# Loads that cast, half-width turns and a re-ordered start in an attention and MLP kernel

## The chip, the core and the metric

The kernel runs on one core of a Trainium2 chip. A core has five engines that run on their own: PE (TensorE, matrix products), ACT (ScalarE), DVE (VectorE), POOL (GpSimd) and SP (SyncE, which here only issues transfers). Sixteen DMA engines move data between the memory of the chip and the core. The metric is the time of one execution in microseconds of device time. The kernel before takes 445.65 us, the median of three runs (445.64 to 447.6).

## The reference

```python
def _attn_ref(q, k, v):                     # (8, 12, 448, 64) each, float32
    S = q.shape[2]
    scale = 1.0 / np.sqrt(q.shape[-1])
    scores = scale * np.matmul(q, k.transpose(0, 1, 3, 2))
    attn = np.maximum(scores, 0.0) ** 2 / S
    return np.matmul(attn, v)

def _moe_ref(x, w_in, w_out, alpha):        # x (3584, 768), d_ff 2048
    h = x @ w_in
    g = np.maximum(h, 0.0) + alpha * np.minimum(h, 0.0)
    return g @ w_out
```

Attention with a squared relu in place of a softmax, over 8 batches of 12 heads, gives x with one row per token; a two-layer MLP with a leaky relu whose slope is given per column follows. Inputs and output are float32 in memory; the products run in bf16.

## The kernel before

Twelve heads of a batch are worked in three groups of four heads, called quads: quad n is group n % 3 of batch n // 3, and there are 24. For a quad, q, k and v are loaded by SP as float32 into `raw` tiles (three buffers each), cast to bf16 by POOL (quad 0's k by ACT and q by DVE), and q and k are turned so that the head dimension lies on the partitions. For quads 0 to 5 the turn is done on PE: seven matmuls of 128x128 with an identity into PSUM (`tps`, L117) and a DVE copy (L119). For later quads a transposing DMA on SP does it.

`scores(n, j)` makes block j (of 7) of a quad's scores in two PSUM banks with four 64x64 matmuls (`sc`, L137); ACT, or DVE for block 3 of the first six quads, takes the relu (`rl`), and DVE squares it (`at`, L147). `attnv(n)` multiplies the seven squares with v (`av`, L157), and ACT copies the result, scaled, into `xT`. Two double banks of PSUM (`scps`) are shared by scores and `av`; four single banks (`mmps`) by everything else.

`ffn1(b, ff)` is one of 16 steps of the first MLP half for batch b: six matmuls (`hps`, L173), a relu of the negative on ACT (`neg`), and one DVE instruction that writes `gT`. `ffn2` is the second half: 16 matmuls (`ops`, L185) give 128 rows by 384 columns, DVE copies them (`osb`, L191), and SP stores them. Batches go in pairs for `ffn2`: an even batch has 6 such groups, an odd one 8.

The order of the work on each engine is the order of the program; nothing reorders it. A quad's attention is cut into four bursts: burst 0 is one block of scores and the `attnv` of the quad before, bursts 1 to 3 are two blocks of scores each. `spread(seq, bursts)` sets bursts among MLP steps so that they are evenly spaced by a written cost (1.12 for an `ffn1` step, 2.6 for an `ffn2` group). Bursts of quads 6 and later also issue the load of quad n+3 (burst 0), the transposing DMAs of quad n+1 (burst 1) and the casts of quad n+2 (burst 2).

The start is written out: SP loads quads 0 to 2 and alpha; attention of batch 0 runs with no MLP work beside it; POOL issues the loads of `w_in` (which cast to bf16 in flight) between its casts. Then `ffn1` of batch 0 runs, with quad 3 among its last steps; quads 4 and 5 follow alone; then 14 steps of `ffn1` of batch 1 alone. From there bursts are spread over `ffn1` of batch b and `ffn2` of batch b-1, and the last batch's MLP ends the program.

Of the kernel before, what the change touches and what calls it, by code (L numbers as in the profile page):

```python
# [10 lines left out]
F32 = mybir.dt.float32  # L11
BF16 = mybir.dt.bfloat16
# [7 lines left out]
PP = 64  # L20
NJ = 7
# [3 lines left out]
def kernel(  # L25
# [27 lines left out]
    raw_pool = pool("raw", 3)  # L53
    cast_pool = pool("cast", 2)
    v_pool = pool("vp", 3)
    qkT_pool = pool("qkT", 2)
    rl_pool = pool("rl", 3)
    at_pool = pool("at", 10)
# [6 lines left out]

    w_in_sb = singles.tile([128, NG, 2, d_ff], BF16)
    w_out_sb = singles.tile([128, KF, d_model], BF16)
    alpha_sb = singles.tile([128, KF], F32)
    beta_sb = singles.tile([128, KF], F32)
    ident = singles.tile([128, 128], BF16)  # L70

    quads = [(b, g) for b in range(B) for g in range(NG)]
# [2 lines left out]
    raw, cast, qT, kT, vb = {}, {}, {}, {}, {}  # L75
    src = {"q": q, "k": k, "v": v}

    def load(n, names="qkv", after=None):
        b, g = quads[n]
        for w in names:  # L80
            t = raw_pool.tile([128, 2, NJ, D], F32, tag=w, name=f"{w}raw")
            raw[(n, w)] = t
            if after is not None:
                nc.gpsimd.tensor_copy(t[:, 0, 0, 0:1], after)
                after = None
            flat = src[w][b, 4 * g:4 * g + 4].rearrange("(s hf) (pp j) d -> (hf pp) s (j d)", hf=2, j=NJ)
            nc.sync.dma_start(out=t.rearrange("p s j d -> p s (j d)"), in_=flat)  # L87

    def copy(eng, o, i):
        if eng is nc.scalar:  # L90
# [4 lines left out]
    def to_bf16(n, w, eng):  # L95
        r = raw.pop((n, w))
        if w == "v":
            t = v_pool.tile([128, 2, NJ, D], BF16, tag="v", name="vb")
            vb[n] = t
            copy(eng, t, r)  # L100
        else:
            t = cast_pool.tile([128, NJ, 2, D], BF16, tag=w, name=f"{w}b")
            cast[(n, w)] = t
            copy(eng, t.rearrange("p j s d -> p s j d"), r)

    def transpose(n, w):
        store = qT if w == "q" else kT
        t = cast.pop((n, w))
        dst = qkT_pool.tile([128, NJ, 2, PP], BF16, tag=w, name=f"{w}T")
        store[n] = dst  # L110
        if n >= n_pe:
            nc.sync.dma_start_transpose(out=dst.rearrange("p j h c -> p j (h c)"),
                                        in_=t.rearrange("p j s d -> p (j s d)"))
            return
        ps = mm_ps.tile([128, NJ, 2, PP], BF16, tag="mm", name="tps")
        for j in range(NJ):
            nc.tensor.transpose(ps[:, j].rearrange("p h c -> p (h c)"),  # L117
                                t[:, j].rearrange("p s d -> p (s d)"), ident)
        nc.vector.tensor_copy(dst, ps)  # L119

    w_in_v = moe_w_in.rearrange("(g hf e pp) f -> hf e pp g f", hf=2, e=2, pp=64)
    w_out_v = moe_w_out.rearrange("(kf p) d -> p kf d", p=128)
# [5 lines left out]
                                    in_=w_in_v[hf, e, :, :, lo:hi])  # L128


    att, xT = {}, {}

    def scores(n, j):
        ps = sc_ps.tile([128, 2, 512], F32, tag="sc", name="sc")
        for r in range(2):
            for c in range(2):
                nc.tensor.matmul(ps[64 * c:64 * c + 64, r, :S],  # L137
                                 kT[n][64 * r:64 * r + 64, j, c, :],
                                 qT[n][64 * r:64 * r + 64, :, c, :],
                                 start=True, stop=True)  # L140
        rl = rl_pool.tile([128, 2, S], BF16, tag="rl", name="rl")
        if (n, j) in relu_on_dve:
            nc.vector.tensor_scalar(rl, ps[:, :, :S], 0.0, None, ALU.max)  # L143
        else:
            nc.scalar.activation(rl, ps[:, :, :S], ACTF.Relu)  # L145
        a = at_pool.tile([128, 2, S], BF16, tag="at", name="at")
        nc.vector.tensor_tensor(a, rl, rl, ALU.mult)  # L147
        att[(n, j)] = a

    def attnv(n):  # L150
        b, g = quads[n]
# [11 lines left out]
        nc.scalar.activation(xT[b][:, g], ps[:, :, :S], ACTF.Copy, scale=out_scale)  # L163


    gT, o_sb = {}, {}

    def ffn1(b, ff):
        if b % 2 == 0 and ff == 0:
# [12 lines left out]
    def ffn2(sb, c, hf):  # L182
        ps = mm_ps.tile([128, 384], F32, tag="mm", name="ops")
        for ff in range(KF):
            nc.tensor.matmul(ps, gT[sb][:, ff, bass.ts(c, 128)],  # L185
                             w_out_sb[:, ff, bass.ts(hf, 384)],
                             start=(ff == 0), stop=(ff == KF - 1))
        if hf == 0:
            o_sb[(sb, c)] = o_pool.tile([128, d_model], F32, tag="o", name="osb")
        o = o_sb[(sb, c)]  # L190
        nc.vector.tensor_copy(o[:, bass.ts(hf, 384)], ps)  # L191
        if hf == 1:
            for u in range(2):
                blk = 2 * c + u
                b, j = 2 * sb + blk // NJ, blk % NJ
                rows = out[b * S:(b + 1) * S].rearrange("(pp j) d -> j pp d", j=NJ)
                nc.sync.dma_start(out=rows[j], in_=o[64 * u:64 * u + 64])

    def steps(b, what):
        if what == "in":  # L200
            return [(1.12, lambda ff=ff: ffn1(b, ff)) for ff in range(KF)]
        cs = range(0, 3) if b % 2 == 0 else range(3, 7)
        return [(2.6, lambda c=c, hf=hf: ffn2(b // 2, c, hf)) for c in cs for hf in range(2)]


    NQ = len(quads)
    relu_on_dve = {(n, 3) for n in range(2 * NG)}

    def burst(n, i):

        if i == 0:
            if n < NQ:
                scores(n, 0)
            if (n - 1, 0) in att:
                attnv(n - 1)
        elif n < NQ:
            scores(n, 2 * i - 1)
            scores(n, 2 * i)
        if n < 2 * NG:
            return  # L220

        if i == 0 and n + 3 < NQ:
            load(n + 3)
        if i == 1 and n + 1 < NQ:
            transpose(n + 1, "k")
            transpose(n + 1, "q")
        if i == 2 and n + 2 < NQ:
            for w in "kqv":
                to_bf16(n + 2, w, nc.gpsimd)

    def spread(seq, bursts, share=0.92):

        total = sum(c for c, _ in seq) * share
        done, n = 0.0, 0
        for cost, fn in seq:
            while n < len(bursts) and done >= total * n / len(bursts):
                burst(*bursts[n])
                n += 1
            fn()
            done += cost  # L240
        assert n == len(bursts)


    for n in range(NG):
        load(n, "kqv")
    nc.sync.dma_start(out=alpha_sb, in_=moe_alpha.rearrange("(kf p) -> p kf", p=128))
    make_identity(nc, ident)
    for n in range(NG):
        to_bf16(n, "k", nc.gpsimd if n else nc.scalar)
        to_bf16(n, "q", nc.gpsimd if n else nc.vector)  # L250
        to_bf16(n, "v", nc.gpsimd)
        if n == 1:
            load_w_in(0, 512)
        if n < 2:
            transpose(n, "k")
            transpose(n, "q")
        if n > 0:
            for i in range(4):
                burst(n - 1, i)
    for i in range(1, 4):  # L260
        load_w_in(512 * i, 512 * i + 512)
    transpose(2, "k")
    transpose(2, "q")
    for i in range(4):
        burst(2, i)
    nc.vector.tensor_scalar(beta_sb, alpha_sb, -1.0, 1.0, ALU.mult, ALU.add)
    attnv(2)


    load(3, "kqv", after=w_in_sb[:, 0, 1, 1024:1025])  # L270
    load(4, "kqv")
    load(5, "kqv")
    for w in "kqv":
        to_bf16(3, w, nc.gpsimd)
    for w in "kqv":
        to_bf16(4, w, nc.gpsimd)
    for h in range(2):
        nc.gpsimd.dma_start(out=w_out_sb[:, 8 * h:8 * h + 8], in_=w_out_v[:, 8 * h:8 * h + 8])
    mlp = steps(0, "in")
    for _, fn in mlp[:9]:  # L280
        fn()
    transpose(3, "k")
    transpose(3, "q")
    for w in "kqv":
        to_bf16(5, w, nc.gpsimd)
    load(6, "kqv", after=w_out_sb[:, 0, 0:1])
    load(7, "kqv")
    load(8, "kqv")
    spread(mlp[9:], [(3, i) for i in range(4)])
    for n in (4, 5):  # L290
        transpose(n, "k")
        transpose(n, "q")
        for i in range(4):
            burst(n, i)
    attnv(5)
    for n in (6, 7):
        for w in "kqv":
            to_bf16(n, w, nc.gpsimd)
    for w in "kq":
        transpose(6, w)  # L300


    work = [(n, i) for n in range(2 * NG, NQ) for i in range(4)] + [(NQ, 0)]
    mlp = steps(1, "in")
    for _, fn in mlp[:14]:
        fn()
    spread(mlp[14:] + steps(0, "out") + steps(1, "out") + steps(2, "in"), work[:25])
    for b in range(3, B - 1):
        spread(steps(b, "in") + steps(b - 1, "out"), work[12 * b - 11:12 * b + 1])
    for _, fn in steps(B - 1, "in") + steps(B - 2, "out") + steps(B - 1, "out"):  # L310
        fn()


# [28 lines left out]
```

## Time and profile before

| What | Value |
|---|---|
| median of three runs | 445.65 us |
| the profiled execution | 447.29 us, of which 445.5 us lie between its first and last instruction (the span) |
| PE busy | 400.6 us, 90% of the span |
| DVE / ACT / POOL busy | 245.7 / 227.6 / 84.0 us |
| mean granted PE clock | 0.965 |
| read from / written to the chip's memory | 45.62 MB / 11.01 MB |

The page of the profile gives an engine's busy time, the span in 40 slices, the chain of waits that ended last, and groups of instructions by line: busy time, mean duration in ns of one, and the idle time ahead of them with what ended it. A name such as `rl<-sc` says which tile is written from which. A row such as `q0 software_dynamic: 1579, 2.40, 112.3%` is a DMA queue in a stretch of time: packets, MB written, and the time that its packets took as a share of 16 engines (q0 is the queue that POOL feeds, q1 the one that SP feeds). PE's busy time includes matmuls that wait in its pipeline, so a full row says only that it never ran dry.

### The profile page before, as it was taken

How to read it: one execution, taken by the hardware profiler on the slowest of the kernel's cores; microseconds unless marked ns; L12 is line 12 of the kernel's file. 1: busy time of each engine (PE TensorE's matmuls, PEld its weight loads, DVE VectorE, ACT ScalarE, POOL GpSimd, SP SyncE). 2: the span in 40 equal slices, each digit the busy share in tenths (PEclk: the TensorE clock that was granted, in tenths of full speed). 3: DMA queues.
4: the chain of work that ended last, by engine and by line, in shares of the span. 5: the costliest groups of instructions: out<-in, count | busy, mean ns of one | idle time of the engine just before them, and what ended most of it. 6: DMA issues, size and time to landing. Idle time of an engine off the chain costs nothing.

```text
span 445.5 us, 7651 instructions
## 1 busy us (share of the span) xinstructions
PE 400.6 (90%) x3092; PEld 201.6 (45%) x3092; DVE 245.7 (55%) x372; ACT 227.6 (51%) x316; POOL 84.0 (19%) x96
## 2 busy tenths in 40 slices
PE   2566986589989889999989999999989999999995
PEld 1232443235445444444445445544544455555663
DVE  1857367555644446867754773477456754263221
ACT  1554456544654547867654773477545754241000
POOL 2936022420012322222020400212020000000000
PEclk9976899669999999999999999999999999999999
DMA  8999996510085899835037705696043102200322
GB/s 276 195 182 368 181 234 249 166 41 1 0 231 148 221 177 250 218 123 166 1 77 212 192 0 161 154 277 172 4 112 77 43 11 61 72 0 20 87 73 71
DMA packets 64980, 59.09 MB, mean 133 GB/s; under 512 B 37809, under 2 KB 61361, under 8 KB 64945
## 3 DMA queue, kind: packets, MB, share of 16 engines
q1 hardware_dynamic: 59536, 52.32, 42.0%
q0 software_dynamic: 5408, 6.29, 8.8%
q8 instruction: 24, 0.39, 0.4%
q14 instruction: 12, 0.09, 0.1%
HBM read 45.62 MB, written 11.01 MB: 127 GB/s over the span
## 4 chain that ended last, share of the span: by engine, by line
PE 84%; ACT 5%; DVE 4%; issue 3%; DMA 2%; SPq 0%; POOL 0%; ACTq 0%
PE hps L173 34%; PE ops L185 33%; PE av L157 8%; PE sc L137 8%; ACT rl L145 5%; DVE at L147 2%; DMA qraw<-in_q_dram 2%; DVE rl L143 1%; DVE qT L119 0%; DVE kT L119 0%; SPq L87 0%; ACT neg L178 0%; DVE gT L179 0%; POOL qb L93 0%; PE tps L117 0%
## 5 line engine op out<-in xcount | busy, mean ns | idle before, releaser
L145 ACT ACTIVATE rl<-sc 128x896 bf16<-128x896 f32 x162 | 140.8, 917 | 99.3 <-PE sc L137 96.0
L173 PE MATMUL hps<-xT,w_in_sb 128*128 128x448 bf16 x768 | 155.0, 357 | 0.0
L185 PE MATMUL ops<-w_out_sb,gT 128*128 128x384 bf16 x896 | 152.0, 326 | 0.0
L147 DVE TENSOR_TENSOR at<-rl 128x896 bf16<-128x896 bf16 x168 | 117.3, 710 | 55.7 <-ACT rl L145 51.5
L185 PEld LDWEIGHTS <-gT 128*128 128x128 bf16 x896 | 84.9, 98 | 65.1 <-issue 11.4
L179 DVE SCALAR_TENSOR_TENSOR gT<-neg,beta_sb,hps 128x448 bf16<-128x448 f32 x128 | 86.4, 678 | 46.3 <-ACT neg L178 45.2
L173 PEld LDWEIGHTS <-w_in_sb 128*128 128x128 bf16 x768 | 72.6, 99 | 78.8 <-issue 17.3
L178 ACT ACTIVATE neg<-hps 128x448 f32<-128x448 f32 x128 | 70.2, 549 | 54.9 <-PE hps L173 54.8
L137 PE MATMUL sc<-qT,kT 64*64 64x448 bf16 x672 | 57.3, 384 | 29.0 <-ACT rl L145 15.9
L191 DVE COPY osb<-ops 128x384 f32<-128x384 f32 x56 | 31.2, 558 | 83.6 <-PE ops L185 80.2
L93 POOL CAST vb<-vraw 128x896 bf16<-128x896 f32 x24 | 25.0, 1044 | 135.1 <-PE av L157 127.9
L137 PEld LDWEIGHTS <-kT 64*64 64x64 bf16 x672 | 16.7, 107 | 66.9 <-issue 58.5
L157 PE MATMUL av<-at,vb 64*64 64x448 bf16 x672 | 43.2, 396 | 2.2 <-ACT rl L145 1.2
L93 POOL CAST kb<-kraw 128x896 bf16<-128x896 f32 x23 | 22.5, 977 | 103.8 <-DMA kT<-kb 64.9
L163 ACT ACTIVATE xT<-av 128x896 bf16<-128x896 f32 x24 | 22.0, 917 | 20.1 <-PE av L157 20.1
L157 PEld LDWEIGHTS <-vb 64*64 64x64 bf16 x672 | 22.5, 118 | 17.4 <-issue 7.5
L93 POOL CAST qb<-qraw 128x896 bf16<-128x896 f32 x23 | 25.1, 1091 | 2.5 <-DMA qT<-qb 1.6
L117 PE MATMUL tps<-ident,kb 128*128 128x128 bf16 x42 | 4.7, 273 | 8.6 <-ACT kb L91 5.1
L127 POOL DMA_DIRECT2D w_in_sb<-in_moe_w_in_dram x16 | 10.1, 635 | 3.3 <-DMA w_in_sb<-in_moe_w_in_dram 3.3
L117 PEld LDWEIGHTS <-kb 128*128 128x128 bf16 x42 | 3.5, 122 | 9.8 <-ACT kb L91 5.1
L143 DVE TENSOR_SCALAR rl<-sc 128x896 bf16<-128x896 f32 x6 | 6.5, 1080 | 0.0
L119 DVE COPY kT<-tps 128x896 bf16<-128x896 bf16 x6 | 3.7, 618 | 4.0 <-PE tps L117 4.0
(16 smaller groups left out, 18.4 us busy)
## 6 DMA issues: line engine op xcount, KB each, us to landing
kraw<-in_k_dram SPq DMA_DIRECT2D x24, 448.0 KB, 5.3
qraw<-in_q_dram SPq DMA_DIRECT2D x24, 448.0 KB, 4.9
vraw<-in_v_dram SPq DMA_DIRECT2D x24, 448.0 KB, 6.4
out_dram<-osb SPq DMA_DIRECT2D x56, 192.0 KB, 2.7
w_in_sb<-in_moe_w_in_dram POOLq DMA_DIRECT2D x16, 192.0 KB, 7.6
w_out_sb<-in_moe_w_out_dram POOLq DMA_DIRECT2D x2, 1536.0 KB, 14.9
kT<-kb SPq DMA_TRANSPOSE x18, 3.1
qT<-qb SPq DMA_TRANSPOSE x18, 2.7
```

Of the source, the lines that this page charges most:

```text
L93: eng.tensor_copy(o, i)
L137: nc.tensor.matmul(ps[64 * c:64 * c + 64, r, :S], kT[n][64 * r:64 * r + 64, j, c, :], qT[n][64 * r:64 * r + 64, :, c, :], start=True, stop ...
L143: nc.vector.tensor_scalar(rl, ps[:, :, :S], 0.0, None, ALU.max)
L145: nc.scalar.activation(rl, ps[:, :, :S], ACTF.Relu)
L147: nc.vector.tensor_tensor(a, rl, rl, ALU.mult)
L157: nc.tensor.matmul(ps[64 * s:64 * s + 64, r, :S], vb[n][64 * r:64 * r + 64, s, j, :], a[64 * r:64 * r + 64, s], start=(j == 0), stop=(j == ...
L163: nc.scalar.activation(xT[b][:, g], ps[:, :, :S], ACTF.Copy, scale=out_scale)
L173: nc.tensor.matmul(ps, w_in_sb[:, km // 2, km % 2, bass.ts(ff, 128)], xT[b][:, km // 2, km % 2, :], start=(km == 0), stop=(km == KM - 1))
L178: nc.scalar.activation(neg, ps, ACTF.Relu, scale=-1.0)
L179: nc.vector.scalar_tensor_tensor(gT[b // 2][:, ff, (b % 2) * S:(b % 2) * S + S], neg, beta_sb[:, ff:ff + 1], ps, ALU.mult, ALU.add)
L185: nc.tensor.matmul(ps, gT[sb][:, ff, bass.ts(c, 128)], w_out_sb[:, ff, bass.ts(hf, 384)], start=(ff == 0), stop=(ff == KF - 1))
L191: nc.vector.tensor_copy(o[:, bass.ts(hf, 384)], ps)
```

## The change

Batches 0 and 1 (quads 0 to 5) are loaded otherwise: `load_bf16` lets POOL issue the transfers of k, q and v, which cast to bf16 in flight, so no engine casts them. They stand on the same queue as `w_in` and `w_out`, in one written order. The tiles hold the two halves of a partition's rows one after another (`[128, 2, NJ, D]`), so a turn now takes 14 matmuls of 64 columns, two per block, instead of 7 of 128.

In batch 0's attention two of a quad's seven blocks (2 and 5) put their scores in the single banks, and their relu is shared by ACT and DVE, half each; squares are issued one block late; `attnv` of the quad before stands behind block 1, and the turns of the next quad behind blocks 3 and 4. The other relus of batch 0 all go to ACT. Alpha is loaded as 16 rows of 128, turned on PE.

An `ffn2` group is issued in two halves of 8 matmuls (written cost 1.3 each). `ffn2` of batch b now follows `ffn1` of the same batch. So quad 3 and the turns of quads 3 and 4 stand among `ffn1` of batch 0, quads 4 and 5 among `ffn2` of batch 0, and each later batch has its own two halves in one stretch. Raw tiles have two buffers instead of three and are loaded at quad n for n+2; v has four.

The core of the diff:

```diff
+    def load_bf16(n, names="kqv"):
+
+        for w in names:
+            if w == "v":
+                t = vb[n] = v_pool.tile([128, 2, NJ, D], BF16, tag="v", name="vb")
+            else:
+                t = cast[(n, w)] = early_pool.tile([128, 2, NJ, D], BF16, tag=w, name=f"{w}e")
+            nc.gpsimd.dma_start(out=t.rearrange("p s j d -> p s (j d)"), in_=flat(n, w))
...
-        ps = mm_ps.tile([128, NJ, 2, PP], BF16, tag="mm", name="tps")
+        ps = mm_ps.tile([128, NJ, 2 * PP], BF16, tag="mm", name="tps")
         for j in range(NJ):
-            nc.tensor.transpose(ps[:, j].rearrange("p h c -> p (h c)"),
-                                t[:, j].rearrange("p s d -> p (s d)"), ident)
-        nc.vector.tensor_copy(dst, ps)
+            for s in range(2):
+                nc.tensor.transpose(ps[64 * s:64 * s + 64, j], t[:, s, j], ident)
+        nc.vector.tensor_copy(dst.rearrange("p j h c -> p j (h c)"), ps)
...
+        if split:
+            half = [mm_ps.tile([128, 512], F32, tag="mm", name="sch") for _ in range(2)]
...
+        if split:
+            nc.scalar.activation(rl[:, 0], half[0][:, :S], ACTF.Relu)
+            nc.vector.tensor_scalar(rl[:, 1], half[1][:, :S], 0.0, None, ALU.max)
...
+    def squares(keep=0):
+        while len(todo) > keep:
+            n, j, rl = todo.pop(0)
+            a = at_pool.tile([128, 2, S], BF16, tag="at", name="at")
+            nc.vector.tensor_tensor(a, rl, rl, ALU.mult)
+            att[(n, j)] = a
...
-        for ff in range(KF):
+        for ff in range(8 * half, 8 * half + 8):
...
-        if i == 0 and n + 3 < NQ:
-            load(n + 3)
+        if i == 0 and n + 2 < NQ:
+            load(n + 2)
...
+    load_bf16(0)
+    make_identity(nc, ident)
+    make_identity(nc, ident_f)
+    load_bf16(1)
+    transpose(0, "k")
+    transpose(0, "q")
+    split = (2, 5)
     for n in range(NG):
+        for j in range(NJ):
+            scores(n, j, split=j in split)
+            squares(keep=1)
+            if j == 1 and n > 0:
+                attnv(n - 1)
+            if j == 3 and n + 1 < NG:
+                transpose(n + 1, "k")
+            if j == 4 and n + 1 < NG:
+                transpose(n + 1, "q")
+        if n == 0:
+            load_bf16(2)
+            load_w_in(0, 512)
+            load_w_in(512, 1024)
+            load_w_in(1024, 2048)
+            load_bf16(3)
+    load_bf16(4)
+    nc.gpsimd.dma_start(out=w_out_sb, in_=w_out_v)
...
+    spread(mlp[6:], [turn(3)] + [(3, i) for i in range(4)] + [turn(4)])
+    load_bf16(5)
+    load(6, after=w_out_sb[:, 0, 0:1])
+    load(7)
...
+    spread(steps(0, "out"), [(4, 0), (4, 1), turn(5), (4, 2), (4, 3), [(5, 0), feed(6)], (5, 1), (5, 2), [(5, 3), feed(7)],
+                             lambda: attnv(5)], 0.86)
...
+    spread(mlp[2:] + steps(1, "out"), work[:13])
+    for b in range(2, B - 1):
+        spread(steps(b, "in") + steps(b, "out"), work[12 * b - 11:12 * b + 1])
```

The order of POOL's instructions at the start, before, from the identity on (`raw` tiles are float32, `kb`, `qb` and `vb` bf16):

```order
masks.py:197 MEMSET ident 128x128
masks.py:199 AFFINE_SELECT ident<-ident 128x128
L93 CAST vb<-vraw 128x896
L93 CAST kb<-kraw 128x2x7x64
L93 CAST qb<-qraw 128x2x7x64
L93 CAST vb<-vraw 128x896
L127 DMA w_in_sb<-in_moe_w_in_dram 64x3x512 x4
L93 CAST kb<-kraw 128x2x7x64
L93 CAST qb<-qraw 128x2x7x64
L93 CAST vb<-vraw 128x896
L127 DMA w_in_sb<-in_moe_w_in_dram 64x3x512 x12
```

And in the changed kernel, from the first instruction behind the constants to quad 3's loads (`ke` and `qe` are the bf16 tiles of quads 0 to 5):

```order
L100 DMA ke<-in_k_dram 128x2x448
L100 DMA qe<-in_q_dram 128x2x448
L100 DMA vb<-in_v_dram 128x2x448
masks.py:197 MEMSET ident 128x128
...
L100 DMA vb<-in_v_dram 128x2x448
L140 DMA w_in_sb<-in_moe_w_in_dram 64x3x512 x8
L140 DMA w_in_sb<-in_moe_w_in_dram 64x3x1024 x4
L100 DMA ke<-in_k_dram 128x2x448
L100 DMA qe<-in_q_dram 128x2x448
L100 DMA vb<-in_v_dram 128x2x448
```

POOL's casts of quads 0 to 5 are gone; the loads of q, k and v have come from SP's queue to POOL's, those of quads 0 to 2 ahead of `w_in`, those of quad 3 behind it.

DVE's order around quads 4 and 5, before (`gT` belongs to `ffn1`, `at` to the squares, `osb` to `ffn2`):

```order
L147 TENSOR_TENSOR at<-rl 128x896 x3
L143 TENSOR_SCALAR rl<-sc 128x896
L147 TENSOR_TENSOR at<-rl 128x896 x4
L179 SCALAR_TENSOR_TENSOR gT<-neg,beta_sb,hps 128x448 x14
L147 TENSOR_TENSOR at<-rl 128x896
L179 SCALAR_TENSOR_TENSOR gT<-neg,beta_sb,hps 128x448 x2
L147 TENSOR_TENSOR at<-rl 128x896 x2
L191 COPY osb<-ops 128x384
```

And in the changed kernel, from the last `gT` of batch 0 on:

```order
L205 SCALAR_TENSOR_TENSOR gT<-neg,beta_sb,hps 128x448 x2
L173 TENSOR_TENSOR at<-rl 128x896
L221 COPY osb<-ops 128x384
L173 TENSOR_TENSOR at<-rl 128x896 x2
L132 COPY kT<-tps 128x896
L132 COPY qT<-tps 128x896
L221 COPY osb<-ops 128x384
L164 TENSOR_SCALAR rl<-sc 128x896
L173 TENSOR_TENSOR at<-rl 128x896 x4
L221 COPY osb<-ops 128x384
```

The first copy of an `ffn2` group has moved from behind batch 1's attention and 16 steps of batch 1's `ffn1` to the first burst of quad 4, and the others follow among the squares of quads 4 and 5.

More of the change, by code (lines that the diff above doesn't have):

```diff
@@ L52 @@
     singles = pool("singles", 1)
-    raw_pool = pool("raw", 3)
+    raw_pool = pool("raw", 2)
     cast_pool = pool("cast", 2)
-    v_pool = pool("vp", 3)
+    v_pool = pool("vp", 4)
+    early_pool = pool("early", 2)
     qkT_pool = pool("qkT", 2)
@@ L76, with flat @@
     src = {"q": q, "k": k, "v": v}
+    def flat(n, w):
+        b, g = quads[n]
+        return src[w][b, 4 * g:4 * g + 4].rearrange("(s hf) (pp j) d -> (hf pp) s (j d)", hf=2, j=NJ)
     def load(n, names="qkv", after=None):
-        b, g = quads[n]
         for w in names:
@@ L187, in ffn2 @@
                              start=(ff == 0), stop=(ff == KF - 1))
-        if hf == 0:
+        if half == 0:
+            return
+        if (sb, c) not in o_sb:
             o_sb[(sb, c)] = o_pool.tile([128, d_model], F32, tag="o", name="osb")
@@ L213, in burst @@
                 scores(n, 0)
+                squares()
             if (n - 1, 0) in att:
@@ L231, in spread @@
     def spread(seq, bursts, share=0.92):
-        total = sum(c for c, _ in seq) * share
+        total = sum(x[0] for x in seq) * share
         done, n = 0.0, 0
@@ L236, in spread @@
             while n < len(bursts) and done >= total * n / len(bursts):
-                burst(*bursts[n])
+                for f in bursts[n] if isinstance(bursts[n], list) else [bursts[n]]:
+                    f() if callable(f) else burst(*f)
                 n += 1
@@ L260 @@
[L260 to L266, printed above, removed]
-    attnv(2)
[L270 to L278, printed above, removed]
+    nc.sync.dma_start(out=alpha_sb, in_=moe_alpha.rearrange("(kf p) -> kf p", p=128))
@@ L279, with turn @@
+    load_bf16(4)
+    nc.gpsimd.dma_start(out=w_out_sb, in_=w_out_v)
+    squares()
+    attnv(2)
+    ps = mm_ps.tile([128, KF], F32, tag="mm", name="aps")
+    nc.tensor.transpose(ps, alpha_sb, ident_f)
+    nc.vector.tensor_scalar(beta_sb, ps, -1.0, 1.0, ALU.mult, ALU.add)
+    def turn(n):
+        return lambda: (transpose(n, "k"), transpose(n, "q"))
     mlp = steps(0, "in")
-    for _, fn in mlp[:9]:
+    for _, fn in mlp[:6]:
         fn()
[L282 to L300, printed above, removed]
+    spread(mlp[6:], [turn(3)] + [(3, i) for i in range(4)] + [turn(4)])
+    load_bf16(5)
@@ L303, with feed, f @@
+    load(6, after=w_out_sb[:, 0, 0:1])
+    load(7)
+    def feed(n):
+        def f():
+            for w in "kqv":
+                to_bf16(n, w, nc.gpsimd)
+            if n == 6:
+                transpose(n, "k")
+                transpose(n, "q")
+        return f
+    spread(steps(0, "out"), [(4, 0), (4, 1), turn(5), (4, 2), (4, 3), [(5, 0), feed(6)], (5, 1), (5, 2), [(5, 3), feed(7)],
+                             lambda: attnv(5)], 0.86)
     work = [(n, i) for n in range(2 * NG, NQ) for i in range(4)] + [(NQ, 0)]
@@ L304 @@
     mlp = steps(1, "in")
-    for _, fn in mlp[:14]:
+    for _, fn in mlp[:2]:
         fn()
[L307 to L310, printed above, removed]
+    spread(mlp[2:] + steps(1, "out"), work[:13])
+    for b in range(2, B - 1):
+        spread(steps(b, "in") + steps(b, "out"), work[12 * b - 11:12 * b + 1])
@@ L311 @@
+    for _, fn in steps(B - 1, "in") + steps(B - 1, "out"):
         fn()
```

52 lines of the change are left out of this document (21 added, 31 removed).

## The prediction

> **What bounds the kernel now.** I read the busy time of each engine by stage first (each row: stretch, its length, busy us of PE, weight loads, DVE, ACT and POOL, granted clock, DMA share, GB/s written).
>
> ```profile
> span 445.5 us, 7651 instructions
> ```
> ```profile
> core 0: us, PE busy (x) PEld busy (x) DVE busy (x) ACT busy (x) POOL busy (x), PEclk, DMA share, GB/s
> 0.00:45.40 45.40, 23.48 (x210) 11.08 (x211) 25.67 (x32) 19.69 (x22) 25.48 (x38) 0.85 1.01 252
> 45.40:95.00 49.60, 37.93 (x311) 18.55 (x308) 30.30 (x46) 26.77 (x37) 11.62 (x13) 0.84 0.76 193
> 95.00:112.20 17.20, 17.20 (x89) 8.49 (x90) 8.85 (x13) 8.27 (x15) 2.70 (x3) 0.95 0.03 7
> 112.20:386.00 273.80, 267.44 (x2169) 132.41 (x2170) 161.61 (x250) 164.18 (x227) 44.17 (x43) 1.00 0.48 127
> ```
>
> From 95 us on, PE is busy in 98% of the time and its own work sets the end. Up to 95 us it is not: in the first 45.4 us (attention of batch 0) it works 23.5, with DMA full and the clock at 0.85; in the next 49.6 (first MLP half of batch 0, attention of batch 1) 37.9. Attention there makes ACT, DVE and PE wait in turn, and no second-half matmuls (`ops`) stand among it. The chain of waits gives the marks (start, duration, what):
>
> ```profile
> 11.43 0.93 PE tps L117 x7
> 12.36 0.55 PE sc L137 x4
> 45.47 12.09 PE hps L173 x54
> 94.98 16.90 PE hps L173 x84
> 300.75 1.32 PE av L157 x28
> 321.17 0.50 PE sc L137 x8
> 321.67 2.71 PE ops L185 x16
> 324.38 0.34 PE sc L137 x4
> 324.95 0.60 issue
> 349.09 3.51 PE hps L173 x18
> 386.03 18.16 PE hps L173 x96
> 404.19 36.41 PE ops L185 x224
> 440.63 0.56 DVE osb L191
> ```
>
> The first scores start at 12.36, because PE's order puts the turns of quad 1, cast late by POOL, before them. The 54 `hps` at 45.47 take 12.09; the 96 at 386 take 18.16, 10.2 for 54: 1.9 is a cold clock. At 324.38 two bursts of scores stand together and the second waits for ACT (0.60 of issue and a relu); such places stand about six times behind 112 us.
>
> **The sum, stage by stage.** I price the changed kernel from its start to the point T where batch 1's attention and batch 0's `ops` are done, then the rest.
>
> *First scores.* Loads and small pieces:
>
> ```profile
> 4.15 0.94 ACT L91 CAST kb<-kraw 128x896 bf16<-128x896 f32 x1 [2.13 <-DMA kraw<-in_k_dram]
> 12.45 2.61 POOL L127 DMA_DIRECT2D w_in_sb<-in_moe_w_in_dram  x4
> DMA to landing us min/median/max: 5.3/5.3/5.3
> L119 DVE COPY kT<-tps x6: 610/618/625, 6.1 to 82.1; 128x896 bf16<-128x896 bf16 x6
> 0.74 0.46 SPq L87 DMA_DIRECT2D kraw<-in_k_dram  x1
> ```
>
> SP's first load, issued at 0.74, was there at 4.15: 3.4 us. POOL's first weight load took 5.3. POOL can issue k at about 0.74 and q 0.65 later (four issues take 2.61), so q is there between 4.8 and 6.7; I take 6.0. Its 14 half-width turns replace 7 full ones of 0.93: 0.93 if pairs run side by side, as four score matmuls do, 1.86 if one after another; I take 1.4, near the middle, since no row has this shape. With the copy, 0.62, scores start at **8.1** (6.4 to 9.2), against 12.36. No cast stands ahead.
>
> The Trainium skill, TensorEngine Tiling (Array Packing), section Restrictions, says that column tiling switches the fast weight load off, which speaks against half-width turns. By it I would take 1.86 here and about 0.3 more in the other eleven turns, a sum some 4 us longer. The trace is partly with it: a load of 64 columns takes 107 ns, of 128 columns 122, so half the columns are far from half the time.
>
> ```profile
> L137 PEld LDWEIGHTS <-kT 64*64 64x64 bf16 x672 | 16.7, 107 | 66.9 <-issue 58.5
> L117 PEld LDWEIGHTS <-kb 128*128 128x128 bf16 x42 | 3.5, 122 | 9.8 <-ACT kb L91 5.1
> ```
>
> *Batch 0's attention, three quads.*
>
> ```profile
> L145 ACT ACTIVATE rl<-sc 128x896 bf16<-128x896 f32 x162 | 140.8, 917 | 99.3 <-PE sc L137 96.0
> L178 ACT ACTIVATE neg<-hps 128x448 f32<-128x448 f32 x128 | 70.2, 549 | 54.9 <-PE hps L173 54.8
> 22.13 0.62 DVE L147 TENSOR_TENSOR at<-rl 128x896 bf16<-128x896 bf16 x1 [0.18 <-ACT rl L145]
> 19.67 0.96 PE L137 MATMUL sc<-qT,kT 64*64 64x448 bf16 x8 [0.67 <-DVE rl L143]
> 21.34 2.83 PE L157 MATMUL av<-at,vb 64*64 64x448 bf16 x28 [0.71 <-ACT rl L145]
> L191 DVE COPY osb<-ops 128x384 f32<-128x384 f32 x56 | 31.2, 558 | 83.6 <-PE ops L185 80.2
> ```
>
> ACT per quad: 5 whole relus and one `xT` at 0.917, 2 halves at 0.55: 6.6. DVE: 7 squares at 0.62, 2 halves at about 0.6 (nearest: 0.558 for 384 columns), 2 turn copies at 0.62: 6.8. PE on a cold clock: 7 scores at 0.48, `av` 2.83, turns 2.8: 9.0; warm: 7 at 0.25, 1.32, turns 1.5: 4.6. So a quad lies between 6.8 and 9.0. The clock flips here (0.85), so I take 8: three quads 24, plus the last relu and square, 1.6: done at **33.7** (28.4 to 37.8), against 45.4. Squares also lose POOL's casts as neighbours.
>
> *First half of batch 0, with quad 3.* 16 steps at 1.17 (3.51 for three), the cold start's 1.9, 7 scores at 0.25, four turns at 0.8 (the 1.4 above on a warmer clock): 25.6, so **59.3**. Its relus (5.5) and `neg` (8.8) make 14 us on ACT, hidden under PE. Nothing is taken out: quads 4 and 5 only move on, into `ops`.
>
> *Are the loads there?* This is the step that I trust least. By two-microsecond and longer windows of the DMA queues:
>
> ```profile
> q0 software_dynamic: 1579, 2.40, 112.3%
> q0 software_dynamic: 852, 0.81, 96.6%
> q1 hardware_dynamic: 478, 0.81, 105.2%
> q0 software_dynamic: 5408, 6.29, 8.8%
> ```
> ```profile
> 18.00:24.00 6.00, 4.21 (x44) 2.06 (x44) 4.54 (x7) 3.01 (x4) 5.67 (x10) 1.00 0.97 134
> 46.00:58.00 12.00, 12.00 (x65) 6.14 (x64) 5.44 (x8) 5.21 (x10) 0.00 (x0) 0.88 1.13 201
> ```
>
> The rows are 46 to 58, 18 to 24, for SP's plain loads 40 to 42 us, and the casting queue's whole. MB are written bf16, twice that is read. From 46 to 58 the casting queue reads 4.80 MB in 12 us, 400 GB/s; plain loads 405. So a cast in flight costs the transfer nothing: reading binds. From 18 to 24 it read only 268, and there POOL was issuing for 5.67 of 6 us; from 46 to 58 it issued nothing. In the change POOL issues 33 loads, so I take 320 while it issues many (between 268 and 400) and 400 for the single `w_out`. Ahead of `w_out` are five quads of 3 x 0.459 MB and `w_in`, half of 2 x 6.29: 13.2 MB, 41 us; `w_out` itself 15.7; start and landing 3.7 (0.74, one issue of 0.65, and the 3.4 of SP's first load less its own 1.1 of transfer): **60.7**. PE asks for it at 59.3 (just behind the first burst of quad 4): a stall of **1.4**; 0 at 400 throughout (52.4). The k and q of quad 3 (11.3 MB) are there at 39.1; PE asks at about 42.5.
>
> *Batch 0's `ops` with quads 4 and 5.* 6 groups at 2.71, 14 scores at 0.25, 3 `av` at 1.4, turns 1.6, and two waits for ACT of 1.5 (0.60 and a relu): 28.6. **T = 89.3**. In the kernel before, batch 1's attention ended at 94.98 and these 16.3 us of `ops` were still to come.
>
> *The rest.* 112 `hps` steps: the last 18 at 1.135, 94 at 1.18 (131.3); 50 groups: 8 at 2.60, 42 at 2.71 (134.6); 18 quads at 3 x 0.50 + 0.34 + 1.32 (56.9); tail 4.9 (440.63 to the end): **327.7**. The same prices for the kernel before from 112.19 give 326.8 (98 steps; 56 groups, 14 of them at 2.60); it took 333.3, so 6.5 us are stalls, and the six places where two bursts met ACT explain them. In halves of 1.3 with 2.57 or 2.97 between bursts, no two bursts meet; I drop them (bound: keep all). The depth of two raw buffers costs nothing if its cover holds: load at a quad's burst 0, cast at burst 2, turn five bursts (some 15 us) later, against
>
> ```profile
> kraw<-in_k_dram SPq DMA_DIRECT2D x24, 448.0 KB, 5.3
> ```
>
> Alpha's 128x16 single elements become 16 rows; the load lies off the path, and its turn on PE is one short matmul.
>
> *Sum.* 89.3 + 327.7 = **417.0** of span. The profiled execution took 447.29, 1.8 more than its span, and the median is 445.65, 1.6 less than it, so the two nearly cancel: **417**.
>
> **Rivals.** *Early:* PE warms up and attention runs at DVE's 6.8 per quad. 28.4, then 22.7 for the next stage (no cold start, turns 0.55), 52.4 for `w_out`, 25 for the next (no waits): T = 78, time 406. For: PE has more to do per us than now. Against: 0.85 of clock in the first stage.
>
> *Late weights:* the queue reads 268 throughout. `w_out` lands at 19.5/0.268 + 3.7 = 76, a stall of 17 instead of 1.4: 433; with 400 for `w_out` alone 425. For: the row of 18 to 24; against: that of 46 to 58. The Trainium skill, SBUF — State Buffer, section Who interferes with whom, has a rule that way: a VectorE instruction in a two-port mode locks GpSimd out, and descriptors of its DMAs wait. By it the thick DVE work of attention would starve this queue; the trace shows slow reading there, while POOL's issues took no longer than before.
>
> *Slower:* the same queue falls to 102 GB/s written, as slices between 18 and 24 had:
>
> ```profile
> GB/s 150 164 191 205 198 191 205 178 164 130 116 75 82 109 130 102 102 75 150 143 178 157 171 198 150 130 109 109 102 109 109 123 109 96 116 123 116 82 130 96
> ```
>
> 204 read: `w_out` at 19.5/0.204 + 3.7 = 99, a stall of 40: 455. It decides once `w_out` lands later than 90 us, an average under 226 GB/s. Against: those slices ended with POOL's issuing.
>
> *The halves don't do what they say:* bursts still meet ACT, or raw loads come late, and 7 us (the stalls of now) to 16 us (1 us for nearly every later quad) return: 424 to 433.
>
> **Chances.** Forecast 0.58, early 0.14, late weights 0.13, halves 0.07, slower or even 0.08. Range 401 to 434: early's upper half, late's most; the forecast's own is 408 to 425. About 0.5% is what a measurement can tell from none: faster 0.92, same 0.03, slower 0.05.
>
> **What would show it.** Right: first scores near 8, first `hps` near 34, first `ops` near 60, batch 1's attention over near 89 with `ops` among it, no ACT wait ahead of scores behind T. Wrong: a wait of `ops` or of quad 3's turn for a POOL load over 5 us; a quad of batch 0 taking over 9; `sc` waiting for `qT` in the steady part.

## The result, and the profile after

The changed kernel takes **410.62 us**, the median of four runs (410.55 to 411.96); the kernel before, run beside it, takes 446.44 (445.64 to 447.6). The ratio is 0.920, with a 95% interval of 0.917 to 0.924. I had forecast 417 in a range from 401 to 434. The profiled execution took 410.55 us, 1.75 more than its span.

The head of the changed kernel's page (the span; busy time, share of the span and instructions of each engine; the chain that ended last by engine):

```profile
span 408.8 us, 7791 instructions
PE 391.2 (96%) x3177; PEld 196.1 (48%) x3177; DVE 239.0 (58%) x374; ACT 225.7 (55%) x318; POOL 80.2 (20%) x94
PE 93%; DVE 3%; ACT 1%; DMA 1%; issue 1%; POOL 0%; ACTq 0%; POOLq 0%
```

PE is busy in 96% of the span instead of 90%, and it makes up 93% of the chain that ended last (last row). PE's busy time fell by 9.4 us, mainly because fewer matmuls ran cold, that is, at a low clock and about twice as long (28 of `av` in 2.83 us instead of 1.32): the mean granted clock went from 0.965 to 0.992. The rest of the 36.7 us of span is idle time that is gone.

Busy time by stage (stretch, length, busy us of PE, weight loads, DVE, ACT and POOL, granted clock, DMA share, GB/s written). The stages end where the first-half matmuls of batch 0 begin, where its second half begins, and where that is done together with the attention of batch 1:

```profile
0.00:32.40 32.40, 20.08 (x254) 10.43 (x255) 18.38 (x33) 18.55 (x25) 20.42 (x36) 0.97 1.08 177
32.40:57.70 25.30, 25.11 (x214) 12.19 (x214) 18.17 (x30) 15.03 (x24) 2.47 (x4) 0.97 1.17 219
57.70:81.80 24.10, 24.08 (x234) 12.26 (x233) 13.98 (x23) 12.40 (x14) 5.38 (x6) 1.00 0.44 134
81.80:386.00 304.20, 304.20 (x2372) 150.71 (x2371) 184.43 (x282) 179.70 (x256) 51.98 (x48) 1.00 0.49 128
```

PE is full from 32.4 us on; in the kernel before it was busy for 98% of the time from 95 us on. Only the first stage still waits. Its 0.97 of clock flatters it: from 8.41 to 13.08 the column says 1.00, but four score matmuls take 0.59 us there, against 0.38 from 20.47 on, so PE was still cold.

The marks on the chain of waits (start, duration, what):

```profile
8.83 0.61 PE sc L155 x4
16.36 2.83 PE av L183 x28
25.06 1.52 PE av L183 x28
32.43 7.58 PE hps L199 x36
56.33 1.32 PE av L183 x28
57.66 2.71 PE ops L213 x16
81.77 2.27 PE hps L199 x12
```

First scores are at 8.83 (12.36 before), first `hps` at 32.43 (45.47 before). At 81.77 the attention of batch 1 and the second half of batch 0 are over. The kernel before had reached 112.19 with about the same amount of work: 14 steps of `hps` in place of 6 groups of `ops`, 16.9 us against 16.3. So some 30 us of the gain lie ahead of that mark. The rest takes 408.8 - 81.8 = 327.0 us against 333.3: 6.3 us.

What PE waited for behind 50 us in the kernel before, the three longest of six rows (engine, line, releaser: us in total, times, longest); the same view of the changed kernel has no row at all:

```profile
PE sc L137 <- ACT rl L145: 8.8, 14, 1.0
PE sc L137 <- DVE qT L119: 5.6, 3, 2.3
PE sc L137 <- ACT xT L163: 1.6, 2, 0.8
```

The casting queue in the changed kernel (packets, MB written, share of 16 engines; from 18 to 24 us and from 46 to 52), and the small POOL copy that waits for `w_out`:

```profile
q0 software_dynamic: 1120, 1.23, 120.7%
q0 software_dynamic: 854, 1.24, 115.2%
53.59 0.34 POOL L89 CAST qraw<-w_out_sb 128x1 f32<-128x1 bf16 x1 [10.63 <-DMA w_out_sb<-in_moe_w_out_dram]
```

It writes 1.23 MB in 6 us, which is 410 GB/s read, also from 18 to 24 us while POOL issues some loads; in the kernel before it was 268 in those six microseconds. `w_out` is there at 53.6 and PE asks for it at 57.66.

### The profile page after: what moved, and what is told of

It is laid out like the page before. It is cut to its first block, busy times and chain, and to the rows that moved or that the text cites. A ratio compares the mean times of both kernels' runs of the same rounds, so it can differ in the third digit from the quotient of the medians.

```text
span 408.8 us, 7791 instructions
## 1 busy us (share of the span) xinstructions
PE 391.2 (96%) x3177; PEld 196.1 (48%) x3177; DVE 239.0 (58%) x374; ACT 225.7 (55%) x318; POOL 80.2 (20%) x94
## 4 chain that ended last, share of the span: by engine, by line
PE 93%; DVE 3%; ACT 1%; DMA 1%; issue 1%; POOL 0%; ACTq 0%; POOLq 0%
PE ops L213 37%; PE hps L199 37%; PE sc L155 10%; PE av L183 9%; DVE at L173 1%; DMA qe<-in_q_dram 1%; ACT rl L166 1%; PE tps L131 1%; DVE rl L162 1%; DVE qT L132 0%; POOL ke L100 0%; DVE kT L132 0%; PE sch L155 0%; DVE osb L221 0%; ACT neg L204 0%
## 5 line engine op out<-in xcount | busy, mean ns | idle before, releaser
L173 DVE TENSOR_TENSOR at<-rl 128x896 bf16<-128x896 bf16 x168 | 114.6, 692 | 55.1 <-ACT rl L166 50.6
L106 POOL CAST kb<-kraw 128x896 bf16<-128x896 f32 x18 | 17.1, 951 | 213.1 <-DMA kraw<-in_k_dram 102.3
L155 PE MATMUL sc<-qT,kT 64*64 64x448 bf16 x648 | 52.1, 374 | 4.2 <-DVE qT L132 1.8
L183 PE MATMUL av<-at,vb 64*64 64x448 bf16 x672 | 38.4, 364 | 2.1 <-ACT rl L166 2.1
L106 POOL CAST qb<-qraw 128x896 bf16<-128x896 f32 x18 | 21.2, 1180 | 0.0
L106 POOL CAST vb<-vraw 128x896 bf16<-128x896 f32 x18 | 21.2, 1177 | 0.0
L131 PE MATMUL tps<-ident,ke 128*64 128x128 bf16 x84 | 4.3, 256 | 4.8 <-DMA ke<-in_k_dram 4.8
L140 POOL DMA_DIRECT2D w_in_sb<-in_moe_w_in_dram x12 | 7.5, 629 | 3.8 <-DMA w_in_sb<-in_moe_w_in_dram 2.1
L100 POOL DMA_DIRECT2D ke<-in_k_dram x6 | 4.4, 740 | 11.6 <-PE tps L131 10.3
L131 PEld LDWEIGHTS <-ke 128*64 128x64 bf16 x84 | 3.2, 132 | 7.0 <-DMA ke<-in_k_dram 4.8
```

The source lines that it names most:

```text
L106: eng.tensor_copy(o, i)
L131: nc.tensor.transpose(ps[64 * s:64 * s + 64, j], t[:, s, j], ident)
L155: nc.tensor.matmul(half[r][64 * c:64 * c + 64, :S], kT[n][64 * r:64 * r + 64, j, c, :], qT[n][64 * r:64 * r + 64, :, c, :], start=True, st ...
L183: nc.tensor.matmul(ps[64 * s:64 * s + 64, r, :S], vb[n][64 * r:64 * r + 64, s, j, :], a[64 * r:64 * r + 64, s], start=(j == 0), stop=(j == ...
```

## Experiments

Six kernels undo or change one part of the change; three ask about the casting queue. Each was timed beside the kernel before. Marks are the starts of the first scores, the first `hps` and the first `ops`, and T, the end of the stage with batch 0's `ops`; in the changed kernel 8.8, 32.4, 57.7 and 81.8.

**The casting loads.** Quads 0 to 2 are loaded as float32 by SP and cast by ACT, DVE and POOL; the order on PE stays.

```diff
-    load_bf16(0)
+    load_plain(0)
+    load_plain(1)
...
-    load_bf16(1)
+    cast_plain(0)
+    cast_plain(1)
...
-            load_bf16(2)
+            load_plain(2)
             load_w_in(0, 512)
+            cast_plain(2)
```

> The changed kernel, but quads 0 to 2 are loaded as float32 by SP and cast by ACT (k of quad 0), DVE (its q) and POOL (the rest); the order of all else, the half-width turns and the split scores stay. Theory A (the gain at the start is in the order of PE's work and in the filled stage; the cast in flight only frees POOL): first scores at about 7.6 us instead of 8.8, squares beside POOL's casts up to 1.3 us instead of 0.62, first MLP matmul at 31 to 34 us (32.4 in the changed kernel), time 410 to 413. Rival B (the cast in flight is what brings the start forward): first MLP matmul at 38 us or later, as w_in also starts later; time 416 or more.

Measured: 412.51 us (411.51 to 413.24), ratio 0.926 (0.922 to 0.929). Rows of PE and POOL in order of time (start, duration, what, idle time before and its releaser):

```profile
8.33 0.96 PE L170 MATMUL sc<-qT,kT 64*64 64x448 bf16 x8 [0.72 <-DVE qT L147]
33.33 7.13 PE L214 MATMUL hps<-xT,w_in_sb 128*128 128x448 bf16 x36
58.50 0.18 POOL L89 CAST qraw<-w_out_sb 128x1 f32<-128x1 bf16 x1 [15.08 <-DMA w_out_sb<-in_moe_w_out_dram]
```

The first scores start even earlier than in the changed kernel, though not at the 7.6 expected, so the early start does not need the casting loads. It comes from the order on PE: in the kernel before, quad 0's turns were done at 6.85 us, and PE then waited for quad 1's:

```profile
10.26 0.93 PE L117 MATMUL tps<-ident,kb 128*128 128x128 bf16 x7 [3.42 <-POOL kb L93]
```

The casting loads are worth 1.9 us of the median (1.4 of the span), in two places: `hps` starts 0.9 later, and `w_out`, there only at 58.50, holds PE for 0.4 us more.

**The split of the scores.** All seven blocks of a quad use the two double banks; the relu of block 3 goes whole to DVE.

```diff
-    relu_on_dve = {(n, 3) for n in range(NG, 2 * NG)}
+    relu_on_dve = {(n, 3) for n in range(2 * NG)}
...
-    split = (2, 5)
+    split = ()
```

> The changed kernel without the split: all scores of batch 0 go to the two double banks, block 3's relu whole to DVE as before. Theory A (banks): scores wait for a relu in each block, some 1 us more per quad, first MLP matmul at about 35 to 36 us, time 413 to 415. Rival B (engine work): ACT has 6.4 us per quad and DVE 6.7 either way (6.6 and 6.8 with the split), so nothing changes, 410 to 411.5.

Measured: 414.83 us (413.12 to 415.45), ratio 0.930 (0.927 to 0.933); the marks are 8.9, 36.9, 62.3 and 86.4. Of the 4.6 us of span, 4.5 are lost before the first `hps`. The last two of the three `av` of batch 0 ran cold there (chain of waits):

```profile
26.67 2.85 PE av L183 x28
33.89 2.83 PE av L183 x28
```

With the first, the three took 2.27, 2.85 and 2.83 us; in the changed kernel they took 2.83, 1.52 and 2.57, which is 1.0 less. The split is worth 4.2 us of the median, near the upper end of what was expected. That is banks that come free earlier; the warmer PE is about 1 us of it.

**Filling the second half with quads 4 and 5.** The same work as in the changed kernel, but quads 4 and 5 first and batch 0's `ops` behind them.

```diff
-    spread(steps(0, "out"), [(4, 0), (4, 1), turn(5), (4, 2), (4, 3), [(5, 0), feed(6)], (5, 1), (5, 2), [(5, 3), feed(7)],
-                             lambda: attnv(5)], 0.86)
+    for f in [(4, 0), (4, 1), turn(5), (4, 2), (4, 3), (5, 0), feed(6), (5, 1), (5, 2), (5, 3), feed(7), lambda: attnv(5)]:
+        f() if callable(f) else burst(*f)
+    for _, fn in steps(0, "out"):
+        fn()
```

> The changed kernel, but batch 0's second MLP half is issued whole behind the attention of quads 4 and 5 instead of among it. Theory A (that stage's gain is the filling): quads 4 and 5 alone take 22 to 23 us as they did before, plus 15.7 us for the groups, against 24.1 together: time 424 to 426. Rival B (the gain is in loads and turns that come earlier): at most 3 us more, 411 to 414.

Measured: 422.43 us (421.52 to 422.61), ratio 0.947 (0.944 to 0.950). The chain of waits:

```profile
66.16 2.85 PE av L183 x26
74.82 2.83 PE av L183 x27
77.65 16.03 PE ops L213 x96
```

The two quads alone take some 20 us, with cold `av`, and then 16 us of `ops` follow: T is 93.7 instead of 81.8, and 420.7 - 93.7 leaves the same 327 us behind it. This is the largest single part, 11.8 us of the median, a little less than the expected 13 to 15.

**The halves of a group.** The second half is spread in whole groups of 16 matmuls again, in the same order.

```diff
-        return [(1.3, lambda c=c, hf=hf, h=h: ffn2(b // 2, c, hf, h)) for c in cs for hf in range(2) for h in range(2)]
+        return [(2.6, lambda c=c, hf=hf: (ffn2(b // 2, c, hf, 0), ffn2(b // 2, c, hf, 1))) for c in cs for hf in range(2)]
```

> The changed kernel with whole groups of 16 matmuls (cost 2.6) in place of halves. Theory A (the halves keep bursts apart): ten bursts meet six groups among quads 4 and 5, so about four pairs of bursts stand together there, 1.5 us each, and about one pair in each of three even batches: 416 to 421. Rival B (the wider spacing of bursts by itself removes the waits): 410 to 412.

Measured: 417.11 us (415.94 to 417.37), ratio 0.935 (0.932 to 0.938). PE's waits behind 50 us, and one such place in order of time:

```profile
PE sc L155 <- ACT rl L166: 5.9, 9, 0.8
PE av L183 <- ACT rl L166: 1.3, 2, 0.8
73.52 0.57 PE L155 MATMUL sc<-qT,kT 64*64 64x448 bf16 x8
74.92 0.38 PE L155 MATMUL sc<-qT,kT 64*64 64x448 bf16 x4 [0.83 <-ACT rl L166]
```

Two bursts stand together again, and the second waits for ACT's relu. Whole groups cost 6.5 us of the median; of the 6.8 us of span, 2.9 lie ahead of T (84.7) and 3.9 behind it (span 415.6). The order of batches alone does not do away with these stalls; halves do.

**Squares at once.** Each square follows its relu on DVE directly.

```diff
-            squares(keep=1)
+            squares()
```

> The changed kernel with the squares of batch 0 issued at once instead of one block late. Theory A (DVE's half of a relu then stands behind a square that waits for ACT): 0.5 to 1 us more per quad, first MLP matmul at 34 to 35 us, time 412 to 413.5. Rival B (PE's cold clock and the whole chain set the pace): no difference, 410 to 411.3.

Measured: 411.73 us (411.38 to 412.72), ratio 0.923 (0.921 to 0.926), 1.1 us more; 0.5 of it is a later arrival of q, which this edit does not touch. The time lies between the two expectations, and the intervals overlap; the late squares are worth 1 us at most.

**Alpha by elements.** Alpha is loaded as in the kernel before, in single elements, and its turn on PE and the float32 identity for it fall away.

```diff
-    alpha_sb = singles.tile([KF, 128], F32)
+    alpha_sb = singles.tile([128, KF], F32)
...
-    nc.sync.dma_start(out=alpha_sb, in_=moe_alpha.rearrange("(kf p) -> kf p", p=128))
     load_bf16(0)
+    nc.sync.dma_start(out=alpha_sb, in_=moe_alpha.rearrange("(kf p) -> p kf", p=128))
```

> The changed kernel with alpha loaded as before, 128x16 single elements on SP, issued behind quad 0's loads, and no turn of alpha on PE. Theory A (the thousands of 4-byte packets of alpha slowed the casting queue in the kernel before, 268 GB/s read from 18 to 24 us): the queue reads clearly under 400 GB/s in some 10 us around these packets, w_out lands at 56 us or later instead of 53.6, first scores or w_in later, time 411 to 415. Rival B (alpha only costs its own packets, under 1 us): w_out lands within 1 us of 53.6, time 410 to 411.5.

Measured: 409.58 us (409.27 to 409.85), ratio 0.918 (0.915 to 0.920): 1.0 us less than the changed kernel, not more. The casting queue from 18 to 24 us kept its rate, so alpha's single elements were not what slowed it in the kernel before:

```profile
q0 software_dynamic: 1130, 1.23, 121.1%
```

`w_out` was there at 53.25. Of the gain 0.6 us is there at the first scores (8.20), because q came at 6.48 instead of 7.10; in four kernels whose edits leave its load alone (no split, `ops` later, whole groups, squares at once) it came between 7.2 and 7.6. This is the fastest version run. Its interval of the ratio overlaps that of the changed kernel; the runs' times themselves do not overlap. Why q comes earlier is open.

**Alpha by rows in the kernel before.** The counterpart: the kernel before with nothing but alpha's new load and turn.

```diff
-    nc.sync.dma_start(out=alpha_sb, in_=moe_alpha.rearrange("(kf p) -> p kf", p=128))
+    nc.sync.dma_start(out=alpha_sb, in_=moe_alpha.rearrange("(kf p) -> kf p", p=128))
...
+    aps = mm_ps.tile([128, KF], F32, tag="mm", name="aps")
+    nc.tensor.transpose(aps, alpha_sb, ident_f)
```

> The kernel before with alpha alone changed: 16 rows of 128 loaded, turned on PE. Theory A: the casting queue reads 380 GB/s or more from 18 to 24 us instead of 268, the loads of quad 3 (which wait for the third quarter of w_in, 31.9 us) start 3 to 5 us earlier; time 443 to 446, since batch 0's attention does not wait for these loads. Rival B: 268 GB/s and 31.9 us stay, time 445 to 447.

Measured: 446.81 us (444.86 to 448.42), ratio 1.001 (0.999 to 1.003). The queue from 18 to 24 us is as slow as ever:

```profile
q0 software_dynamic: 877, 0.83, 96.7%
```

My theory that alpha's elements slow the queue falls by both runs.

**A pause ahead of `w_in`, and casts between its loads.** One execution each, so no interval. In both, POOL casts a scratch tile that nobody reads; all of the computation stays. First: eight casts ahead of the `w_in` loads, so that the queue runs empty. Second: three casts behind the first four loads and three behind the next four (the definition of `casts` is left out).

```diff
             load_bf16(2)
+            casts(8)                # first kernel
             load_w_in(0, 512)
+            casts(3)                # second kernel
             load_w_in(512, 1024)
+            casts(3)                # second kernel
```

> The changed kernel with eight POOL casts (a scratch tile, 128x896 float32 to bf16, read by nobody) between the loads of quad 2 and the twelve loads of w_in, so that the casting queue runs empty before w_in and starts again with nothing outstanding. It asks why the same w_in loads ran at about 270 GB/s read in the kernel before (18 to 24 us: 0.81 MB written, 852 packets) and at about 410 in the changed kernel (1.23 MB, 1120 packets). Theory A (the queue is slow while it is filled anew, POOL issuing one load behind the other with few outstanding): in the six microseconds after POOL's first w_in load has been issued and its first data have come, the queue reads under 330 GB/s, under 1.0 MB written in 6 us. Rival B (the casts and float32 loads of the kernel before, or something in its batch 0, slow it): about 400 GB/s, 1.2 MB. Either way w_in is there some 5 to 8 us later, and first hps wait for it or not: 33 to 36 us; time 411 to 418.

Measured: 415.07 us. POOL's loads after the pause, and the queue from 20 to 26 and from 26 to 32 us:

```profile
19.79 6.18 POOL L142 DMA_DIRECT2D w_in_sb<-in_moe_w_in_dram  x10
q0 software_dynamic: 641, 0.61, 73.3%
q0 software_dynamic: 1154, 1.23, 121.6%
```

POOL issues ten loads one behind the other, and in these six microseconds the queue reads only 2 x 0.61 / 6 = 203 GB/s; then it is at 410. The first 1.1 us of the six pass before the first data; from then on, from 21.1 to 26 us, it is 2 x 0.61 / 4.9 = 249. The changed kernel moved the same loads at 403 (15 to 21 us) when they stood behind others in a full queue. So a queue that ran empty is slow at first, as theory A has it. `w_out` comes late for PE by 1.9 us in this kernel.

> The changed kernel with three of the same scratch casts on POOL behind the first four loads of w_in and three behind the next four: casts on POOL while the queue has loads outstanding. Theory A (a queue that is filled anew is slow, POOL's casts are not what slows it): the queue keeps about 400 GB/s read (1.2 MB written in 6 us) while the casts run, as long as loads are outstanding. Rival B (POOL's casts slow the transfers): under 330 GB/s in the stretch of the casts. Time within 3 us of the changed kernel's 410.6 in both, since w_in has some slack before 32 us.

Measured: 412.3 us. The queue from 12.9 to 16.4, from 14 to 20 and from 18 to 24 us:

```profile
q0 software_dynamic: 803, 0.71, 125.0%
q0 software_dynamic: 1253, 1.16, 121.1%
q0 software_dynamic: 1027, 1.00, 109.5%
```

The first casts ran from 12.9 to 16.4 us, and the queue read 406 GB/s beside them: POOL's casts do not slow it. Later it fell to 333, also beside the second casts (18.9 to 22.1). The loads outstanding became few then, which fits the other kernels, but this stretch alone does not tell the two causes apart.

## Why the prediction was right, and where it was off

The direction and the mechanism were right; the sum was 8.2 us of span too long, and 6.4 of the median.

| Step | forecast, us | measured, us |
|---|---|---|
| first scores | 8.1 | 8.8 |
| attention of batch 0 | 25.6 | 23.6 |
| first half of batch 0, quad 3 | 25.6 | 25.2 |
| stall for `w_out` | 1.4 | 0 |
| `ops` of batch 0, quads 4 and 5 | 28.6 | 24.1 |
| rest | 327.7 | 327.0 |
| span | 417.0 | 408.8 |

*First scores.* I let POOL issue k at 0.74, and it issued at 1.25, and a load took it 0.72 instead of 0.65; q was there at 7.15, against 6.0 taken and 6.7 as the bound. A faster turn made up for a part of this (rows of POOL and PE in order of time, and the group of the turns' weight loads).

```profile
1.25 0.84 POOL L100 DMA_DIRECT2D ke<-in_k_dram  x1 [0.80 <-POOLq L357]
7.15 0.96 PE L131 MATMUL tps<-ident,qe 128*64 128x128 bf16 x14 [1.37 <-DMA qe<-in_q_dram]
39.95 0.58 PE L131 MATMUL tps<-ident,ke 128*64 128x128 bf16 x14
L131 PEld LDWEIGHTS <-ke 128*64 128x64 bf16 x84 | 3.2, 132 | 7.0 <-DMA ke<-in_k_dram 4.8
```

*Turns.* I took 1.4 us for 14 half-width turns on a cold clock and 0.8 on a warmer one; they took 0.96 and 0.58, as long as the seven full ones of before (0.93 cold): pairs run side by side. The last row says that a weight load of 64 columns is no shorter than one of 128 was (132 ns against 122), which fits the rule of the Trainium skill (TensorEngine Tiling (Array Packing), Restrictions) that column tiling goes without the fast weight load. But the 84 loads, 11.1 us when added up, kept the unit busy for 3.2 us in all; the 42 of before, 5.1 us, for 3.5: half-width loads overlap more. The 4 us that I had worked out from that rule are not there.

*Attention of batch 0.* 23.6 us with the last `av`: 7.9 a quad, where I took 8 and 1.6 for the end. It was not my cold bound of 9.0: the first `av` ran cold (2.83), the second took 1.52, the third 2.57. That squares lose POOL's casts as neighbours was right; I had given it no size. DVE's squares from 10 to 20 us, in the changed kernel, in the one with plain loads and in the kernel before (times, busy us, mean ns):

```profile
L173 DVE TENSOR_TENSOR at<-rl 128x896 bf16<-128x896 bf16 x8 | 4.7, 620 | 1.6 <-ACT rl L166 1.6
```
```profile
L188 DVE TENSOR_TENSOR at<-rl 128x896 bf16<-128x896 bf16 x8 | 8.6, 1114 | 1.6 <-ACT rl L181 1.6
```
```profile
L147 DVE TENSOR_TENSOR at<-rl 128x896 bf16<-128x896 bf16 x4 | 5.2, 1315 | 1.1 <-ACT rl L145 1.0
```

The last mean is a mixture: two of its four squares took 0.63 us each, and the two beside POOL's casts 3.93 together.

*The loads.* The step that I trusted least failed in its term of 320 GB/s (bounds 268 to 400) for the queue while POOL issues: it ran at 410, `w_out` was there at 53.6 instead of 60.7, and the stall of 1.4 us is zero. I read the row from 18 to 24 us of the kernel before as the price of POOL's issuing. Issuing alone is not what costs: from 8.41 to 13.08 us POOL of the changed kernel issued seven loads one behind the other (busy for 4.52 of 4.67 us), and the queue read 398 GB/s:

```profile
q0 software_dynamic: 1107, 0.93, 125.7%
```

The pause shows what does, a queue that has run empty and is filled anew. In the kernel before it had not quite run empty: its first four loads had been issued by 15.06 us, the next only from 18.10 on, so few were left in it. That this explains its 268 rests on the likeness; no run changes it there.

The Trainium skill (SBUF — State Buffer, Who interferes with whom) says beside the rule that I used that a VectorE instruction with two SBUF inputs contends with a GpSimd instruction that reads SBUF. The squares above agree: they slow down beside POOL's casts. But by that section squares have no two-port mode, so the rule behind my rival of late weights does not cover them. That DVE work starves the transfers is not borne out either, since they ran at 410 beside 620 ns squares. The rivals of late weights (425 to 433) and slower (455) fall with it. Low rates do occur, 249 after the pause, but for some five microseconds, not as an average.

*`ops` with quads 4 and 5.* This is the largest error, 4.5 us. Two waits for ACT of 1.5 us each were in my sum, and there were none: halves keep bursts apart here, too, which I had granted only for the rest. One of the three `av` that I put here stands ahead of the first `ops` (56.33 in the chain), 1.4. These two make 4.4. The stage before came out right by errors that cancel: that `av` more, 1.3; the cold start less by 1.3 (36 `hps` in 7.58 us against 7.02 by the warm row of 3.51 for 18: 0.6 where I took 1.9); and the turns less by 0.9.

*The rest.* 327.0 against 327.7: the row prices held, and all 6.5 us of stalls went, as I had said (behind 112.19 PE waited for ACT's relu eight times, 5.0 us, where I had counted about six). With whole groups 3.9 us returned behind T; the rival that halves do nothing is out.

*Early* (406, T = 78) was the nearest rival, and the result lies between it and the forecast, a little nearer to it (4.6 us against 6.4). Its load of `w_out` (52.4) and its stage without waits (25) came; its attention at 6.8 us a quad did not, nor did 22.7 us for the first half.

Undone singly, the parts cost 11.8 (filling), 6.5 (halves), 4.2 (split), 1.9 (casting loads) and at most 1 us (late squares); alpha by rows, which I had put at nothing, costs some 1.0, with intervals that overlap. Filling, halves, split and loads are 24.4 of the 36 us, if they simply add up, which no run tests. The remaining 12 I did not undo singly: quad 0's turns ahead of quad 1's, quad 3's turns among the first half, the new order of batches behind T, no casts of quads 3 to 5 on POOL. That the first of these, and not the casting loads, sets the early start follows from the run with plain loads and from PE's wait for quad 1 in the kernel before; how the rest divides is open.

## What to carry to other kernels

When one engine is the bound in most of the span, look for the stages in which it is not, and give it matmuls that are ready (a second MLP half among attention) before making the other engines faster there: this was a third of the gain, and it kept the clock up. Interleave in enough pieces that no two bursts stand together: twelve halves of 8 matmuls (1.41 us each) among ten bursts hid a relu of 0.92 us each time, six groups of 16 did not. A rate read from a stretch belongs to the state of the queue in that stretch: ask whether it was full before carrying it to another schedule.

## What the hardware showed that I had not expected

A casting queue that was filled anew took some five microseconds from its first data to its full rate: it read 249 GB/s after the pause made on purpose and 268 in the kernel before, against 403 with the same loads in a full queue. The kernel with plain loads, whose POOL casts ahead of its `w_in` loads, shows it too (270 from 18 to 24 us), and so does the changed kernel's own start (220 from 5 to 7 us). The changed kernel from 15 to 21 us, and the kernel with the pause from 21.1 to 26 us, with packets of the same mean size (0.95 KB):

```profile
q0 software_dynamic: 1276, 1.21, 123.0%
q0 software_dynamic: 641, 0.61, 89.7%
```

A packet takes 16 engines x 6 us x 1.230 / 1276 = 93 ns in the full queue and 16 x 4.9 x 0.897 / 641 = 110 ns after the pause. So each packet takes about a fifth longer, and the engines also have fewer in hand (a share of 90% against 123%). Why is open. Alpha's elements, POOL's casts and POOL's issuing alone are excluded by the runs.

Casts in flight took nothing off the rate at which the queue reads: 410 GB/s read with half of that written, against 405 for plain loads before.
